# An expert layer whose second product moves 384 tokens past stationary weights, in place of 256 weight columns past stationary tokens

## The chip, the cores and the metric

The kernel runs on one core of a Trainium2 chip. The metric is the time of one execution on the device, in microseconds (us). TensorE is written PE in the profile (its weight loads PEld), VectorE DVE, ScalarE ACT, GpSimd POOL, SyncE SP.

## The reference, cut to what matters

Attention with keys and values pooled by 8 gives 2304 tokens of 512 channels, a dense layer pair (512 to 2048 to 512) follows, and then eight experts whose outputs are added under gates. The last part is the one that is changed:

```python
def _moe2_ref(x, w_gate, w1, w2):
    logits = x @ w_gate                       # 2304 x 8
    P = np.exp(logits - logits.max())
    for _ in range(8):
        P /= P.sum(1, keepdims=True) + 1e-09
        P /= P.sum(0, keepdims=True) + 1e-09
        P *= N / E
    out = np.zeros((N, D), dtype=np.float32)
    for e in range(E):                        # 8 experts
        h = np.maximum(x @ w1[e], 0.0)        # 512 -> 1024
        ye = h @ w2[e]                        # 1024 -> 512
        out += P[:, e:e + 1] * ye
    return out
```

## The kernel before

A float32 product is made on PE as three products of halves: each operand is split into a rounded high half and the low rest, and high by high, high by low and low by high are added in PSUM. The high half is a copy to the rounded type, mostly on ACT; the low half is a subtraction (operand less its high half) on DVE or POOL. The expert products moreover use a Strassen-Winograd scheme: seven block products with sums of blocks in place of eight.

The program has four stages: attention; the dense layers, item by item in a list `steps` of first-layer and second-layer pieces (matmuls in L663 and L698); the first pass over the experts; the second pass. Small jobs (the router, the Sinkhorn rounds, the splitting of weights) are generators in a list `side`, from which `advance()` takes one step at a time between products.

**First pass** (class `Unit`, matmul in L878). The tokens are 3 units `u` of 2 times 384. For each pair of 128-channel rows of an expert's hidden layer and each unit there are seven products of six matmuls, with 384 tokens moving. DVE and ACT combine them into seven forms of the hidden layer (B-side and A-side sums of the scheme), which SP writes to `hidden` in DRAM (`hid` in the trace).

**Second pass** (class `Pair`, matmul in L1092). It runs over 8 experts times 9 blocks `s` of 128 tokens, 72 pairs. A pair's forms come back from DRAM (`load_hidden`, tile `hl`), and `prepare` splits each form of 128 x 512: ACT writes the high half `g0` (L1057), and the low half `g1` (L1065) comes from POOL for two of the seven forms, from DVE through a copy in PSUM for three (ACT writes the copy `pg`, L1061), and from DVE straight for two. A product is 12 matmuls: 128 tokens of the form are stationary, 256 columns of `w2` move, and the result is token-major. `read` adds the products' banks (`poa` to `pod`) and `gated` multiplies by the gate, a scalar per partition, and adds to the accumulators `acc` in one instruction (L1109). After the last expert an accumulator is stored as it is (L1156). The seven products run in the order m1, m6, m3 of the pair before, m2, m7, m5, m4. Forms are split `AHEAD = 4` products ahead of their use; at the seam of the passes the first four are prepared by `first_weights` while the last units of the first pass run. The next expert's `w2` is loaded and split by `weights_ahead` (highs on ACT L994, lows on POOL L996, sums on POOL L987) one step for each product.

The very last product of the first pass, `last.product(3)`, follows the first product of the second pass.

Of the kernel before, what the change touches and what calls it, by code (L numbers as in the profile page):

```python
# [17 lines left out]
def tile_attention_mlp_moe(  # L18
# [539 lines left out]
    def gate_tile(t):  # L558
# [17 lines left out]
        yield  # L576
        ps = bank(f"pgt{t}")
# [16 lines left out]
    def sinkhorn():  # L594
# [17 lines left out]
        for it in range(8):  # L612
# [24 lines left out]
            yield  # L637


    side = []  # L640
# [215 lines left out]
    class Unit:  # L856
# [35 lines left out]
        def read(self, m):  # L892
# [7 lines left out]
            elif m == 2:  # L900
                self.r11 = self.temp("r11")
                nc.scalar.activation(self.r11, p["a"], AF.Relu)
                self.keep(H11, self.r11)
            elif m == 7:
                self.u3 = self.temp("u3")
                nc.vector.tensor_add(self.u3, p["b"], self.m1)
# [5 lines left out]
            elif m == 4:  # L912
                self.r12 = self.temp("r12")
                nc.vector.tensor_add(self.r12, p["d"], self.u3)
                nc.scalar.activation(self.r12, self.r12, AF.Relu)
                self.keep(H12, self.r12)
            else:

                c, s2 = p["c"], bank(f"ps_{self.i}_{self.u}")[:, 0:UW]
# [22 lines left out]
    w2s, loaded, prepared, acc = {}, {}, {}, {}  # L942
# [3 lines left out]
    pairs2 = [(e, u, s) for e in range(E) for u in range(NUNIT) for s in range(UB)]  # L946

# [4 lines left out]
    LOADS2 = (range(0, 4), range(4, 7))  # L952


    ON_POOL = (HS2, HS1)
    THROUGH_PSUM = (H11, H12, H22)

    POOLED = (H12, H22, 7 + H11, 7 + H12)
# [16 lines left out]
    def sum_w2(e, j, half):  # L975

        a, b = {T3: (T1, B22), T1: (T1, B11), T2: (B22, T1), T4: (B21, T2)}[j]
        if j == T3:
            if e == 0:
                out = piece([P, 2, HF], F32, f"t3_{half}")  # L980
            else:
                out = half_of(spare[0], half)
# [18 lines left out]
    def weights_ahead(e):  # L1001

        load_w2(e)
        for _ in range(8 if e > 1 else 12):
            yield
        for half in range(2):
            for j in (B11, B22, T3, B21, T1, T2, T4):
                if j in SUMS:
                    sum_w2(e, j, half)
                    yield  # L1010
                    yield
                yield from split_w2(e, j, half, nc.gpsimd)
                yield
                if j not in SUMS:
                    yield

    spare = []

    def last_acc():

        both = slot([P, SLOT], F32, "acc_t3")
        half = SLOT // 2
        acc[NTILE - 1] = both[:, 0:half].rearrange("p (s d) -> p s d", d=DM)
        spare.append(both[:, half:SLOT].rearrange("p (f d) -> p f d", f=NPAIR))

    next_load = [0]

    def load_hidden(forms):

        for _ in range(forms):  # L1030
            n, j = divmod(next_load[0], 7)
            next_load[0] += 1
            if n >= len(pairs2):
                return
            e, u, s = pairs2[n]
# [8 lines left out]
    def prepare(i):  # L1044
        run(prepare_steps(i))
# [465 lines left out]
```

## Time and profile before

| what | value |
|---|---|
| median of 3 runs | 1933.96 us (1933.7 to 1940.49) |
| the profiled execution: its own time | 1934.86 us |
| the profiled execution: span from first to last instruction | 1933.1 us |
| granted TensorE clock | 1.000 of full speed in all 40 slices |
| PE busy | 1906.9 us, 99% of the span |
| DVE, ACT, POOL busy | 70%, 56%, 38% |
| first matmul of the second pass starts | 1195.48 us |
| last group of 12 matmuls starts | 1926.52 us |

The span is the same execution's own time less 1.8 us that lie outside the first and last instruction. Durations below come from this execution. The trace pipelines matmuls: the time that a group of matmuls costs is read from the distance of the starts of two neighbouring groups, not from the printed length.

### The profile page before, as it was taken

The numbers are of one execution on the slowest core, as the hardware profiler recorded it, in microseconds if no ns is written. First come the engines' busy times: TensorE is split into PE (matmuls) and PEld (weight loads), VectorE is DVE, ScalarE is ACT, GpSimd is POOL, SyncE is SP. The second block draws the span as 40 slices with busy tenths as digits, with TensorE's granted clock in tenths as the row PEclk, the third lists the DMA queues.
The fourth block names the chain that finished last, engine by engine and source line by source line (L and its number), as shares of the span: only waits on it lengthen the run. The fifth ranks groups of instructions, "written<-read, shape, count | busy, mean of one in ns | idle before, by whom it ended". The sixth has DMA issues, their size and how long they took to land.

```text
span 1933.1 us, 35728 instructions
## 1 busy us (share of the span) xinstructions
PE 1906.9 (99%) x12635; PEld 1812.7 (94%) x12635; DVE 1356.4 (70%) x2557; ACT 1088.2 (56%) x2241; POOL 741.2 (38%) x658
## 2 busy tenths in 40 slices
PE   6999999999999999999999999999999999999998
PEld 4778888888999999999999999999999999999998
DVE  7778878456787666666666667557777777777766
ACT  7764545344544444444444446776666666666654
POOL 5700000010443333333333327566565656464621
PEclk9999999999999999999999999999999999999999
DMA  9421111000465556665566658876959495958675
GB/s 265 117 98 34 66 44 33 2 10 1 154 221 209 210 199 225 223 218 202 206 225 218 218 197 286 224 210 178 268 154 266 138 265 153 266 157 232 191 202 164
DMA packets 440163, 335.83 MB, mean 174 GB/s; under 512 B 25520, under 2 KB 431024, under 8 KB 439984
## 3 DMA queue, kind: packets, MB, share of 16 engines
q1 hardware_dynamic: 439984, 333.56, 55.8%
q8 instruction: 99, 1.62, 0.3%
q14 instruction: 80, 0.66, 0.1%
HBM read 196.62 MB, written 136.84 MB: 173 GB/s over the span
## 4 chain that ended last, share of the span: by engine, by line
PE 93%; DMA 2%; ACT 1%; POOL 1%; DVE 1%; issue 0%; SPq 0%; DVEq 0%; ACTq 0%; POOLq 0%
PE pb L878 10%; PE pa L878 10%; PE pc L878 10%; PE p L698 10%; PE poa L1092 10%; PE pob L1092 10%; PE poc L1092 10%; PE p L663 10%; PE pd L878 5%; PE pod L1092 5%; DMA hl<-hid 1%; POOL vraw L279 1%; DMA vraw<-in_v_dram 1%; PE px L425 1%; ACT g L1057 0%; PE pt L391 0%
## 5 line engine op out<-in xcount | busy, mean ns | idle before, releaser
L1057 ACT CAST g<-hl 128x512 fp32r<-128x512 f32 x504 | 304.6, 620 | 74.3 <-PE pob L1092 37.3
L1065 POOL TENSOR_TENSOR g<-hl,g 128x512 fp32r<-128x512 f32 x148 | 192.6, 1302 | 303.1 <-ACT g L1057 291.0
L849 POOL TENSOR_TENSOR w<-rw,w 128x512 fp32r<-128x512 f32 (+1 forms) x96 | 139.9, 1489 | 306.5 <-ACT w L847 211.9
L1092 PE MATMUL poa<-w,g 128*128 128x256 f32 x1728 | 232.3, 284 | 2.6 <-ACT n L1119 1.8
L1092 PE MATMUL pob<-w,g 128*128 128x256 f32 x1728 | 231.0, 283 | 0.0
L878 PE MATMUL pa<-xs,w 128*128 128x384 f32 x1152 | 230.9, 334 | 0.0
L1092 PE MATMUL poc<-w,g 128*128 128x256 f32 x1728 | 230.8, 283 | 0.0
L878 PE MATMUL pb<-xs,w 128*128 128x384 f32 x1152 | 230.8, 334 | 0.0
L878 PE MATMUL pc<-xs,w 128*128 128x384 f32 x1152 | 230.6, 334 | 0.0
L1092 PEld LDWEIGHTS poa<-w,g 128*128 128x128 f32 x1728 | 217.7, 192 | 4.9 <-ACT n L1119 3.5
L698 PE MATMUL p<-h,w 128*128 128x512 f32 (+1 forms) x960 | 215.8, 371 | 2.3 <-ACT h L686 1.9
L1092 PEld LDWEIGHTS pob<-w,g 128*128 128x128 f32 x1728 | 217.9, 192 | 0.1
L1092 PEld LDWEIGHTS poc<-w,g 128*128 128x128 f32 x1728 | 217.7, 192 | 0.0
L878 PEld LDWEIGHTS pb<-xs,w 128*128 128x128 f32 x1152 | 202.3, 188 | 0.3 <-DVE u L899 0.3
L878 PEld LDWEIGHTS pa<-xs,w 128*128 128x128 f32 x1152 | 202.2, 188 | 0.2
L878 PEld LDWEIGHTS pc<-xs,w 128*128 128x128 f32 x1152 | 202.4, 188 | 0.0
L698 PEld LDWEIGHTS p<-h,w 128*128 128x128 f32 x960 | 166.7, 189 | 36.8 <-ACT h L686 2.5
L841 POOL TENSOR_TENSOR rw<-rw 128x256 f32<-128x256 f32 x32 | 24.4, 762 | 419.1 <-DMA rw<-in_moe_w_dram 411.2
L1065 DVE TENSOR_TENSOR g<-pg,g 128x512 fp32r<-128x512 f32 x212 | 144.9, 684 | 49.2 <-ACT pg L1061 45.4
L938 ACT COPY s<-pc 128x384 f32<-128x384 f32 x96 | 46.2, 481 | 232.7 <-DVE ps L929 230.8
L663 PE MATMUL p<-xh,w 128*128 128x512 f32 x512 | 170.6, 393 | 0.0
L1065 DVE TENSOR_TENSOR g<-hl,g 128x512 fp32r<-128x512 f32 x144 | 132.7, 922 | 19.1 <-ACT g L1057 13.9
(186 smaller groups left out, 3292.2 us busy)
## 6 DMA issues: line engine op xcount, KB each, us to landing
hl<-hid SPq DMA_DIRECT2D x504, 256.0 KB, 5.2
hid<-s SPq DMA_DIRECT2D x384, 192.0 KB, 2.4
hid<-r SPq DMA_DIRECT2D x288, 192.0 KB, 2.6
rw<-in_moe_w_dram SPq DMA_DIRECT2D x128, 128.0 KB, 2.5
rv<-in_moe_w_dram SPq DMA_DIRECT2D x32, 512.0 KB, 7.1
raw<-in_moe_w_in_dram SPq DMA_DIRECT2D x16, 512.0 KB, 4.3
raw<-in_moe_w_out_dram SPq DMA_DIRECT2D x16, 512.0 KB
vraw<-in_v_dram SPq DMA_DIRECT2D x16, 288.0 KB
```

Source lines behind the costliest of these rows:

```text
L279: ins = nc.gpsimd.tensor_add(x[:, :, 0:n], x[:, :, 0:n], x[:, :, n : 2 * n])
L425: nc.tensor.matmul(ps[h * D : (h + 1) * D, :], vsum_of(u)[:, h * D : (h + 1) * D], turned_of(u, h), start=True, stop=True,)
L663: nc.tensor.matmul(ps[:, 0:n], wc[:, 0, a, c * P : (c + 1) * P], b[:, c, :], start=c == 0 and m == 0, stop=c == NC - 1 and m == 2,)
L698: nc.tensor.matmul(ps[j][:, 0 : WIDTH[t]], wc[:, 1, a, j * P : (j + 1) * P], h[b], start=f == 0 and m == 0, stop=f == SIZE[g] - 1 and m == 2,)
L841: g.tensor_sub(raw[:, S3], raw[:, A11], raw[:, A21])
L849: g.tensor_sub(w1s[i][1][:, js], raw[:, rs], f32(w1s[i][0][:, js]))
L878: nc.tensor.matmul(self.bank[b], a[:, c, :], x, start=first and c == 0 and n == 0, stop=c == 1 and n == 2, skip_group_check=not first,)
L938: nc.scalar.copy(v, x)
L1057: nc.scalar.copy(hi, x)
L1065: eng.tensor_sub(lo, x, f32(hi))
L1092: nc.tensor.matmul(self.bank[b], h[a][:, f, :], w2s[self.e, j][:, l, f, :], start=first and f == 0 and n == 0, stop=f == NPAIR - 1 and n == 2,
```

## The change

**Second pass** (class `Block` in place of `Pair`). It runs over 8 experts times 3 units, 24 blocks. A product's stationary operand is a chunk of 128 output channels of `w2`, and 384 tokens of the form move; the block of 256 channels is two chunks, each with a PSUM bank of its own, so a product is 2 x 12 matmuls and its result is channel-major. Forms are loaded and split in halves of 128 x 768 (two of the four 128-row pieces) in a ring: `load_half` fetches one, `high_half` is one ACT copy (L1088), and `low_half` is one subtraction in place (L1098): 9 of a block's 14 on DVE, 5 on POOL, none through PSUM.

**Gates.** The gate of a token now lies along the free axis. After Sinkhorn, two PE transposes, two ACT copies and 18 small DMAs write the gates as rows to `gate_rows` in DRAM; each block fetches two rows, spread over the 128 partitions (`gr`). `gated` is a multiplication and an addition on DVE (L1150, L1151); for the first expert it is one multiplication on DVE, where before it was an ACT instruction.

**Outputs.** The accumulators are channel-major (128 channels x 384 tokens). In the last expert `turn` transposes each unit's accumulators on PE (L1198), 72 transposes of 128 x 128, ACT copies the result to SBUF (L1204) and it is stored.

**Weights.** `weights_ahead` spreads the next expert's loads, sums and splits over about 42 calls of `advance`, and waits with the last three until the first product of the expert's last unit has been issued.

**Seam and dense layers.** At the seam nothing is split ahead any more; `first_weights` only loads. Two neighbouring entries of `steps` are exchanged, so that the first-layer piece of the last item of the dense layers runs one step earlier. Two more pauses stand in the router's generator, and the first pass releases its banks earlier.

```diff
+        yield from lull()
+        g = gates.rearrange("p s e -> p (s e)")
+        ps = bank("pgr")
+        nc.tensor.transpose(ps[:, 0:P], g[:, 0:P], ident)
+        nc.tensor.transpose(ps[0 : NS * E - P, P : 2 * P], g[:, P : NS * E], ident)
+        rows = piece([P, T], F32, "grows")
...
+                    nc.sync.dma_start(
+                        gate_rows[:, u, th, s * P : (s + 1) * P],
+                        rows[r : r + E, o * P : (o + 1) * P],
+                    )
...
-    ON_POOL = (HS2, HS1)
-    THROUGH_PSUM = (H11, H12, H22)
...
+    POOLED = {(6, 0), (2, 0), (3, 0), (4, 0), (5, 0)}
...
     def weights_ahead(e):
...
+        yield from load(B11, T1, 0)
+        yield from load(B22, B21, 0)
+        yield from load(B11, T1, 1)
+        yield from split(B11)
+        yield from load(B22, B21, 1)
+        yield from split(B22)
+        yield from sums(T3)
+        yield from split(T3)
+        yield from sums(T1, T2)
+        while last_of[0] < e:
+            yield
+        yield from split(T2, B21, T1)
+        yield from sums(T4)
+        yield from split(T4)
...
+    def load_half():
...
+            n, j, half = halves2[i]
+            ring[i] = slot([P, 2, 2, UW], F32R, f"hl{i}")
             nc.sync.dma_start(
...
+                f32(ring[i][:, 1]), hidden[blocks[n]][:, j, 2 * half : 2 * half + 2, :]
             )
...
+    def high_half():
...
+            nc.scalar.copy(ring[i][:, 0], f32(ring[i][:, 1]))
...
+    def low_half():
...
+            hi, lo = ring[i][:, 0], ring[i][:, 1]
+            eng = nc.gpsimd if (j, half) in POOLED else nc.vector
+            eng.tensor_sub(lo, f32(lo), f32(hi))
...
+    class Block:
...
+            for th in range(2):
+                g = piece([P, UW], F32, f"gr{n}_{th}")
+                one = gate_rows[self.e : self.e + 1, self.u, th, :]
+                nc.sync.dma_start(g, bass.AP(one.tensor, one.offset, [[0, P], [1, UW]]))
...
-        def product(self, j):
+        def product(self, j, halves=(0, 1), chunks=(0, 1)):
...
-                        h[a][:, f, :],
-                        w2s[self.e, j][:, l, f, :],
...
+            for half in halves:
+                h = ring[place2[self.n, j, half]]
+                for c in chunks:
+                    for f in range(2):
+                        for n, (l, x) in enumerate(((0, 0), (0, 1), (1, 0))):
+                            nc.tensor.matmul(
+                                self.bank[b][c],
+                                w2s[self.e, j][:, l, 2 * half + f, c * P : (c + 1) * P],
+                                h[:, x, f, :],
...
+        def gated(self, eng, th, dh, c, v):
+            y = self.y(th, dh, c)
             if self.e == 0:
-                nc.scalar.activation(y, v, AF.Copy, scale=gate)
+                eng.tensor_mul(y, v, self.gate[th])
             else:
-                nc.vector.scalar_tensor_tensor(y, v, gate, y, op0=ALU.mult, op1=ALU.add)
...
+                eng.tensor_mul(v, v, self.gate[th])
+                eng.tensor_add(y, v, y)
...
             elif m == 4:
...
+                for c in chunks:
+                    V.tensor_add(p["d"][c], p["d"][c], self.u3[c])
+                    self.gated(V, 1, 0, c, p["d"][c])
...
+        def turn(self, th, dhs=(0, 1), chunks=(0, 1), copy=None):
...
+                        nc.tensor.transpose(
+                            ps[s][:, cols[-1] : cols[-1] + P],
+                            self.y(th, dh, c)[:, s * P : (s + 1) * P],
+                            ident,
+                        )
...
+                (copy or nc.scalar.copy)(sb[:, s, ds], ps[s][:, ds])
...
+                    store(t, r, sb[:, s, :])
...
         steps += [(2, i - LAG)] if i - LAG >= N0 else []
+    ahead = steps.index((1, len(items) - 1))
+    steps[ahead - 1 : ahead + 1] = steps[ahead], steps[ahead - 1]
...
-        ahead = [prepare_steps(next(coming)) for _ in range(AHEAD)]
-        next(ahead[0])
...
     AHEAD = 4
...
+    def multiply(block, j):
...
+        for half in range(2):
+            i = place2[block.n, j, half]
+            last_one = min(i + AHEAD, len(halves2) - 1)
+            while next_low[0] <= last_one:
+                if next_high[0] <= next_low[0]:
+                    high_half()
+                low_half()
+            while next_high[0] <= min(i + AHEAD + 0, len(halves2) - 1):
+                high_half()
+            block.product(j, (half,))
+            load_half()
+            advance()
+        block.read(j)
...
+            for j in (0, 1, 6, 2, 3, 4, 5):
+                if j < 6:
+                    multiply(block, j)
...
+                if n == 0 and j == 0:
+                    last.product(3)
+                    w1s.clear()
...
+                if final and j == 0:
+                    before.turn(1)
+                if final and j == 3:
+                    before.turn(0)
...
+        block.product(6, chunks=(0,))
+        block.turn(1)
+        block.turn(0, dhs=(0,))
+        block.read(6, chunks=(0,))
+        block.product(6, chunks=(1,))
+        block.turn(0, dhs=(1,), chunks=(0,))
+        block.read(6, chunks=(1,))
+        block.turn(0, dhs=(1,), chunks=(1,))
```

ACT at the seam, before: `r22` and `r12` are the last ReLUs of the first pass, `g0` the high halves (number 4 is the fifth form), `n1` the read of the first product.

```order
L910 ACTIVATE r22_31_2_12976<-r22_31_2_12976 128x384
L915 ACTIVATE r12_31_2_12987<-r12_31_2_12987 128x384
L1057 CAST g0_4_12993<-hl0_1_12788 128x512
L1119 COPY n1_0_13010<-poa_0_12997 128x256
L1057 CAST g0_5_13018<-hl0_1_12788 128x512
L938 COPY s1_31_2_13047<-pc_31_2_12969 128x384
```

The same place in the changed kernel, where `hl0`, `hl1` and so on are the half forms and `u20`, `u21` the read of the first product.

```order
L931 ACTIVATE r22_31_2_12983<-r22_31_2_12983 128x384
L936 ACTIVATE r12_31_2_12994<-r12_31_2_12994 128x384
L1088 CAST hl0_12786<-hl0_12786 128x768
L1088 CAST hl1_12798<-hl1_12798 128x768
L1088 CAST hl2_12812<-hl2_12812 128x768
L1088 CAST hl3_12825<-hl3_12825 128x768
L1088 CAST hl4_12874<-hl4_12874 128x768
L1088 CAST hl5_12885<-hl5_12885 128x768
L1159 COPY u20_0_13044<-poa_0_0_13012 128x384
```

The high half that the first product needs stood further up among the first pass's copies; it now stands behind the last ReLU, and six casts stand ahead of the read of the first product.

DVE in the second pass, before: a pair's middle, with the lows `g1` between the reads of the banks.

```order
L1127 TENSOR_TENSOR v3_39_18919<-pob_39_18848,n1_39_18841 128x256
L1065 TENSOR_TENSOR g1_279_18924<-hl39_1_18673,g0_279_18923 128x512
L1130 TENSOR_TENSOR pc_39_18945<-poc_39_18932,v3_39_18919 128x256
L1065 TENSOR_TENSOR g1_282_18949<-pg282_18951,g0_282_18948 128x512
L1132 TENSOR_TENSOR pc_39_18945<-pod_39_18954,v3_39_18919 128x256
L1109 SCALAR_TENSOR_TENSOR acc1_13281<-pc_39_18945,gates_80,acc1_13281 128x512
```

The same products (m5 and m4) of a block in the changed kernel.

```order
L1175 TENSOR_TENSOR pt13_0_16932<-poc_13_0_16898,u30_13_16892 128x384
L1150 TENSOR_TENSOR pt13_0_16932<-pt13_0_16932,gr13_1_16696 128x384
L1151 TENSOR_TENSOR acc2_13501<-pt13_0_16932,acc2_13501 128x384
L1175 TENSOR_TENSOR pt13_1_16936<-poc_13_1_16899,u31_13_16893 128x384
L1150 TENSOR_TENSOR pt13_1_16936<-pt13_1_16936,gr13_1_16696 128x384
L1151 TENSOR_TENSOR acc3_13505<-pt13_1_16936,acc3_13505 128x384
L1098 TENSOR_TENSOR hl196_16889<-hl196_16889 128x768
L1098 TENSOR_TENSOR hl197_16912<-hl197_16912 128x768
L1179 TENSOR_TENSOR pod_13_0_16942<-pod_13_0_16942,u30_13_16892 128x384
L1150 TENSOR_TENSOR pod_13_0_16942<-pod_13_0_16942,gr13_1_16696 128x384
L1151 TENSOR_TENSOR acc2_13501<-pod_13_0_16942,acc2_13501 128x384
```

Each read is now two groups of an addition, a multiplication and an addition of 384 columns, and the two lows between them stand one behind the other.

PE at the end of the program, before: the last product's matmuls.

```order
L1092 MATMUL pod_71_23672<-w2_7_5_21787,g1_502_23606 128x256
L1092 MATMUL poc_71_23657<-w2_7_6_21357,g0_503_23626 128x256 x2
L1092 MATMUL poc_71_23657<-w2_7_6_21357,g1_503_23627 128x256
L1092 MATMUL poc_71_23657<-w2_7_6_21357,g0_503_23626 128x256 x2
L1092 MATMUL poc_71_23657<-w2_7_6_21357,g1_503_23627 128x256
```

The same end in the changed kernel, from the first chunk of the last product; `pt1` and `pt0` are the banks that receive transposes.

```order
L1124 MATMUL poc_23_0_19814<-hl334_19750,w2_7_6_18478 128x384 x6
L1124 MATMUL poc_23_0_19814<-hl335_19770,w2_7_6_18478 128x384 x6
L1198 MATMUL pt1_0_23_19894<-ident_72,acc4_13782 128x128 x4
L1198 MATMUL pt1_1_23_19895<-ident_72,acc4_13782 128x128 x4
L1198 MATMUL pt1_2_23_19896<-ident_72,acc4_13782 128x128 x4
L1198 MATMUL pt0_0_23_19917<-ident_72,acc3_13505 128x128 x2
L1198 MATMUL pt0_1_23_19918<-ident_72,acc3_13505 128x128 x2
L1198 MATMUL pt0_2_23_19919<-ident_72,acc3_13505 128x128 x2
L1124 MATMUL poc_23_1_19815<-hl334_19750,w2_7_6_18478 128x384 x6
L1124 MATMUL poc_23_1_19815<-hl335_19770,w2_7_6_18478 128x384 x6
L1198 MATMUL pt0_0_23_19917<-ident_72,acc3_13505 128x128
L1198 MATMUL pt0_1_23_19918<-ident_72,acc3_13505 128x128
```

18 transposes have come between the two chunks of the last product, and 6 behind it (two of them shown).

## Rows read from the trace of the kernel before

**Rows 1.** The page: busy time, granted clock, DMA share, and the critical chain.
```profile
PE 1906.9 (99%) x12635; PEld 1812.7 (94%) x12635; DVE 1356.4 (70%) x2557; ACT 1088.2 (56%) x2241; POOL 741.2 (38%) x658
...
PEclk9999999999999999999999999999999999999999
...
PE 93%; DMA 2%; ACT 1%; POOL 1%; DVE 1%; issue 0%; SPq 0%; DVEq 0%; ACTq 0%; POOLq 0%
```
**Rows 2.** Stretches of the second pass: PE busy (matmuls), clock, DMA share, GB/s.
```profile
1195.48:1220.00 24.52, 23.72 (x187) 1.00 1.06 328
1220.00:1240.00 20.00, 19.15 (x157) 1.00 1.16 289
...
1300.00:1600.00 300.00, 300.00 (x2502) 1.00 0.77 214
```
**Rows 3.** Timeline of PE, second pass: start, length, instructions.
```profile
1195.48 1.59 PE L1092 MATMUL poa<-w,g 128*128 128x256 f32 x12
...
1500.29 1.60 PE L1092 MATMUL poc<-w,g 128*128 128x256 f32 x12
1501.72 1.60 PE L1092 MATMUL pod<-w,g 128*128 128x256 f32 x12
...
1926.52 1.60 PE L1092 MATMUL poc<-w,g 128*128 128x256 f32 x12
```
**Rows 4.** Timeline of PE, first pass.
```profile
800.95 1.20 PE L878 MATMUL pd<-xs,w 128*128 128x384 f32 x6
801.99 1.20 PE L878 MATMUL pa<-xs,w 128*128 128x384 f32 x6
```
**Rows 5.** A later stretch, busy time and instructions: PE, PEld, DVE, ACT, POOL.
```profile
1500.00:1700.00 200.00, 200.00 (x1669) 200.00 (x1668) 143.44 (x258) 131.74 (x250) 116.17 (x90) 1.00 0.72 200
```
**Rows 6.** Timeline near the seam: ACT's last ReLU of the first pass.
```profile
1196.60 0.53 ACT L915 ACTIVATE r<-r 128x384 f32<-128x384 f32 x1
```
**Rows 7.** Casts on ACT, 560 to 1100 us, by shape: busy, mean ns.
```profile
L847 ACT CAST w<-rw 128x768 fp32r<-128x768 f32 x25 | 21.0, 839 | 26.6 <-PE pc L878 25.5 <-issue 1.0
```
**Rows 8.** DMA issues: KB each, median us from issue to landing.
```profile
hl<-hid SPq DMA_DIRECT2D x504, 256.0 KB, 5.2
```
**Rows 9.** Timeline of PE in the dense layers, the wait in brackets.
```profile
489.74 1.40 PE L698 MATMUL p<-h,w 128*128 128x256 f32 x7 [1.58 <-ACT h L686]
```
**Rows 10.** Timeline of PE in attention: four transposes and what follows.
```profile
64.67 0.60 PE L391 MATMUL pt<-ident,u 128*72 128x128 f32 x4
65.02 1.17 PE L698 MATMUL p<-h,w 128*128 128x512 f32 x4
```
**Rows 11.** Timeline of DVE at the end of the program.
```profile
1928.63 0.48 DVE L1109 SCALAR_TENSOR_TENSOR acc_t<-poc,gates,acc_t 128x256 f32<-128x256 f32 x1
```
**Rows 12.** DVE by shape: the first pass (560 to 1100), the second (1300 to 1900).
```profile
L921 DVE TENSOR_TENSOR pc<-pc,u 128x384 f32<-128x384 f32 x74 | 41.9, 566 | 30.5 <-PE pc L878 30.5
...
L1065 DVE TENSOR_TENSOR g<-pg,g 128x512 fp32r<-128x512 f32 x180 | 123.0, 683 | 23.9 <-ACT pg L1061 21.1 <-POOL g L1065 0.4
L1065 DVE TENSOR_TENSOR g<-hl,g 128x512 fp32r<-128x512 f32 x120 | 110.3, 919 | 0.0
```
**Rows 13.** POOL by shape, 560 to 1100 us, then 1300 to 1900 us.
```profile
L849 POOL TENSOR_TENSOR w<-rw,w 128x768 fp32r<-128x768 f32 x25 | 46.3, 1851 | 171.4 <-ACT w L847 163.4 <-PE pa L878 7.9
...
L1065 POOL TENSOR_TENSOR g<-hl,g 128x512 fp32r<-128x512 f32 x120 | 155.7, 1297 | 248.7 <-ACT g L1057 236.9 <-DMA hl<-hid 11.0
L996 POOL TENSOR_TENSOR w<-rv,w 128x512 fp32r<-128x512 f32 x72 | 93.5, 1299 | 23.7 <-ACT w L994 21.2 <-DMA hl<-hid 1.7 <-DVE g L1065 0.7
```
**Rows 14.** DVE's subtractions that read `hl`: minimum, median, maximum ns.
```profile
L1065 DVE TENSOR_TENSOR g<-hl,g x144: 679/683/1830, 1194.3 to 1921.8; 128x512 fp32r<-128x512 f32 x144
```
**Rows 15.** Timelines of DVE and POOL around 1622 us.
```profile
1621.79 1.61 DVE L1065 TENSOR_TENSOR g<-hl,g 128x512 fp32r<-128x512 f32 x1
...
1621.54 1.30 POOL L996 TENSOR_TENSOR w<-rv,w 128x512 fp32r<-128x512 f32 x1
1622.80 1.75 POOL L987 TENSOR_TENSOR acc_t<-rv,rv 128x512 f32<-128x512 f32 x1
```

More of the change, by code (lines that the diff above doesn't have):

```diff
@@ L1001, in weights_ahead, with rest_for, load @@
     def weights_ahead(e):
[L1003 to L1008 removed]
+        def rest_for(n):
+            for _ in range(n):
+                yield
+        def load(j0, j1, i):
+            if i == 0:
+                both[j0] = slot([P, 2, NPAIR, HF], F32, f"rv{e}_{j0}")
+            j = (j0, j1)[i]
+            hh, dh = {B11: (0, 0), T1: (0, 1), B21: (1, 0), B22: (1, 1)}[j]
+            rows = w2[e][hh * HALF : (hh + 1) * HALF, dh * HF : (dh + 1) * HF]
+            raw2[e, j] = both[j0][:, i]
+            nc.sync.dma_start(both[j0][:, i], rows.rearrange("(f p) d -> p f d", p=P))
+            yield
+            if not i:
+                yield
@@ L1009, in weights_ahead, with split, sums @@
+        def split(*js):
+            for j in js:
+                for half in range(2):
+                    more = split_w2(e, j, half, nc.gpsimd)
+                    next(more)
+                    yield
+                    run(more)
+                    yield
+        def sums(*js):
+            for j in js:
+                for half in range(2):
                     sum_w2(e, j, half)
                     yield
-                    yield
-                yield from split_w2(e, j, half, nc.gpsimd)
@@ L1013, in weights_ahead @@
[L1013 to L1031, printed above, removed]
-            next_load[0] += 1
-            if n >= len(pairs2):
-                return
-            e, u, s = pairs2[n]
-            part = int(j >= LOADS2[1].start)
-            js = LOADS2[part]
-            if j == js.start:
-                loaded[n, part] = slot([P, len(js), NPAIR, P], F32, f"hl{n}_{part}")
+        both = {}
@@ new lines, in product @@
+        def product(self, j, halves=(0, 1), chunks=(0, 1)):
+            m = ORDER2[j]
+            b = PRODUCTS[m][2]
+            first = PRODUCTS[m][3] or m == 7
+            if b not in self.bank:
+                self.bank[b] = [bank(f"po{b}_{self.n}_{c}")[:, 0:UW] for c in range(2)]
+            for half in halves:
[7 more added lines that the diff above has]
+                                h[:, x, f, :],
+                                start=first and half == 0 and f == 0 and n == 0,
+                                stop=half == 1 and f == 1 and n == 2,
+                                skip_group_check=m in (2, 3),
+                            )
+                if chunks[-1] == 1:
+                    del ring[place2[self.n, j, half]]
```

265 lines of the change are left out of this document (119 added, 146 removed).

## The prediction

> **What bounds the kernel now.** I read the busy shares and the clock of the page first: PE is busy 99% of the span at the full granted clock, 2.4 GHz, and holds 93% of the critical chain [rows 1]. So the time is a count of matmuls times what one costs, and the next view is the second pass by stretches. From 1300 to 1600 us PE runs 2502 matmuls in 300.0 us without a gap [rows 2]: 119.9 ns for a matmul with 256 moving columns. Two neighbouring groups of 12 start 1.43 us apart, which is the same [rows 3]. In the first pass, where 384 columns move past the same 128 x 128 weights, groups of six start 1.04 us apart [rows 4]: 173.3 ns. The reader should see that 1.5 times the columns cost 1.445 times the time. The slope is 53.4 ns for 128 columns, 0.417 ns each, which is one column per cycle at 2.4 GHz; what is left, 119.9 - 106.7 = 13.2 ns, is paid once per matmul whatever moves.
>
> The second pass runs from 1195.48 to 1926.52 + 1.44 = 1927.96 us [rows 3]: 732.5 us. Its 72 x 7 x 12 = 6048 matmuls take 725.1 of these, the six of the first pass's last product 1.0, and about 6.3 us are waits. Those lie at the start: the first 44.5 us hold 187 + 157 matmuls, some 41.2 us of work, while the DMA share stands at 1.06 and 1.16 [rows 2].
>
> The other engines have room: between 1500 and 1700 us DVE is busy 72%, ACT 66%, POOL 58% [rows 5].
>
> **The change, part by part.**
>
> *Matmuls.* 24 blocks x 7 products x 24 = 4032 matmuls with 384 columns, in place of 6048 with 256. The columns streamed are the same, 1,548,288; what goes is 2016 times the fixed part. 4032 x 0.1733 = 698.9 against 725.1: **-26.2 us**. The weights' width is 128 columns in both, so the shape is exactly that of the first pass, and the bounds are narrow (13 ns times 2016 is 26.6).
>
> [...]
>
> *Seam.* Before, the first product's operand was split early and PE went on at 1195.48. Now ACT's first cast stands behind the last ReLU, which ends at 1196.60 + 0.53 = 1197.13 [rows 6]. A cast of 768 takes 0.84 [rows 7], the low half behind it 0.92 (below), with hand-overs 1199.1: 3.6 us of wait where there was none. About 1 us more I allow for the following halves, whose casts run at 0.84 us against 2.08 us of PE work each. So about 4.5 us of waits take the place of 6.3: **-1.8 us**. Nothing in the trace shows the ring starting; the bounds are no wait at all (-6.3) and 10 us of it (+3.7), if the loads behind a DMA share over 1 come late (a load takes 5.2 us to land [rows 8], and the ring reads the same bytes).
>
> *Steps of the dense layers.* The exchange removes the one wait of 1.58 us before the second-layer matmuls at 489.74 [rows 9]: **-1.6 us**, or 0 if what ACT has queued there only moves the wait.
>
> *Gate rows.* Four transposes of 128 x 128 advance PE by 0.35 us (64.67 to 65.02) [rows 10], 87.5 ns each; two of them are **+0.2 us**. Their two copies and 18 DMAs, and the 48 loads of 192 KB, lie on ACT and SP some 600 us ahead of the pass, or beside 29 us of PE work; uncovered, one row load would cost as much as a form's load, 5.2 us, once.
>
> *Transposes of the outputs.* 66 stand ahead of the last product's end: 66 x 0.0875 = **+5.8 us**. Twice, in the last two blocks, `turn(1)` follows the next block's first product and needs the accumulations of m4, six DVE operations that are queued behind lows; I take a wait of 1.0 us each, **+2.0 us** (bounds 0.4 and 2.5 each).
>
> *Tail.* Before, from the last matmul's end (1927.96) to the end of the span (1933.1) it is 5.1 us: an addition and a gate on DVE until 1929.11 [rows 11], then 4.0 for the store. Now let T be the end of product m4 of the last block. DVE then has six operations, 3.5 us; 12 transposes 1.1 (T + 4.6), six more 0.5, the second chunk of the last product 2.1 (T + 7.2), its three DVE operations 1.7 (T + 8.9), three transposes and three short ACT copies 0.9 (T + 9.8), and the store 4.0: T + 13.8. With the last product's 4.16 and 1.6 of transposes already counted, 8.0 us are left after them: **+2.9 us** (bounds +1 and +6).
>
> Sum: -26.2 - 1.8 - 1.6 + 0.2 + 5.8 + 2.0 + 2.9 = -18.7. Against the profiled execution, 1934.86 us, that is 1916.2; that execution lies 0.9 above the median of the runs, so 1915.3 on their scale. I predict 1916.
>
> *What must stay hidden.* A block is 168 x 0.1733 = 29.1 us of PE. **DVE** has 26 reads of 384 columns in a block (from the second expert on), 0.566 each by the nearest row [rows 12]: 14.7 us. The scalar gate of one instruction has become a multiplication and an addition, and the copies in PSUM are gone. Its nine lows of 768: 512 columns take 0.683, 384 columns 0.566 [rows 12], so 768 take about 0.92: 8.3 us. That is 23.0 of 29.1, if nothing slows the lows. **POOL** has five lows of 1.85 and a third of the weights' work (14 splits of 1.30 and 8 sums, taken at the same) [rows 13]: 9.3 + 9.5 = 18.8 us, 65%. **ACT** has 14 casts of 0.84 [rows 7], a third of the weights' 14 at no more than that, and two reads of about 0.53 [rows 6]: 11.8 + 3.9 + 1.1 = 16.8. In order, each product needs its halves four halves ahead; the tightest are those issued between the reads of m5 and m4, which are ready about 2 us after product m1 of the following block starts and are needed after 4.2 or later. So none of the three should hold PE, but DVE is the one near it.
>
> *What slows the lows.* A subtraction that reads two SBUF operands has a median of 0.683 and a maximum of 1.83 us [rows 14], a mean of 0.919 where those that read PSUM keep 0.683 [rows 12]. At 1621.79 one took 1.61 us: POOL's split ran to 1622.84, the subtraction ended 0.6 behind it, and POOL's next operation took 1.75 [rows 15], against 1.30 of its neighbours. They exclude one another. The change turns the lows that read PSUM into lows that read SBUF. The mean wait is 0.919 - 0.683 = 0.24 at a POOL share of 58% and operations of 1.30; with 65% and 1.85 it becomes 0.24 x 1.12 x 1.42 = 0.38: 3.4 us a block, DVE at 26.4 of 29.1 us, 91%. It decides at (29.1 - 23.0) / 9 = 0.68 us of wait for each low.
>
> [...]
>
> **The rivals.**
>
> *Small waits in each block* (chance 0.15). Reads now stand in pairs of three operations, so a bank comes free some 1.7 us later than one read of before; with the two lows behind, PE could wait half a microsecond per block. Against it: eight banks and the slack above. 24 x 0.5 = 12 us more: 1928.
>
> *DVE becomes the bound through POOL* (0.08), the case on the other side. If every low meets half a POOL operation, 0.93, DVE needs 14.7 + 9 x 1.85 = 31.4 us a block, 2.3 more than PE; over the 21 blocks that have a gated addition 48 us: 1964. From a wait of 0.68 it binds, and from 0.83 (1.35 us a block, 28.4 in all) the kernel is more than 0.5% slower. For it: the maximum of 1.83 in rows 14. Against: the measured mean.
>
> *The fixed part is not saved* (0.03): 384 columns past `w2` cost 106.7 x 1.5 plus as much as three halves of the fixed part, and only about 5 us come off: 1937. Against it stands the first pass with the same shape.
>
> *Seam or tail are 10 us longer* (0.08), by late loads: 1926.
>
> *Better than forecast* (0.08): no waits at the seam and before the transposes, and a tail as before: 1916.2 - 4.5 - 2.0 - 2.9 = about 1907.
>
> **How the numbers follow.** The forecast, 1908 to 1924 around 1916, has the rest, 0.58. I take 0.5% (9.7 us) as what this kernel's measurement can tell from no change: faster is below 1924.3, slower above 1943.6. Faster gets the forecast, the better case, and the lighter thirds of the small waits and of the seam: 0.70. Slower is the DVE case and a little of the others: 0.10; the rest, 0.20, is the same. The range takes in the forecast, the small waits, the longer seam and the lower end of the bounds: 1908 to 1935, and leaves out half of the better case, the DVE case and part of the fixed-part case.
>
> **What would show it.** Right: groups of six L1124 matmuls 1.04 us apart in the steady part, PE without gaps from about 1205 us on, about 709 us from the first L1124 matmul to the last, no bracketed wait near 490 us, DVE's lows of 768 at 0.92 in the median and below 1.6 in the mean, DVE busy near 90%. Wrong: idle before L1124 released by DVE's L1098 or by its reads (small waits or the DVE bound), by the load of `hl` (seam), or a spacing of six above 1.1 us.

## The result and the profile after

The changed kernel takes 1917.08 us (median of 4 runs, 1914.32 to 1918.23); before, beside it, 1935.65. The ratio is 0.990, 95% interval 0.9888 to 0.9912: faster by 1.0%, clear of the 0.5% that the prediction took as the least that can be told. The prediction was 1916, range 1908 to 1935. The profiled execution has a time of 1917.55 and a span of 1915.8 us, 17.3 shorter than before's.

On the page, PE is busy 1890.2 us (99% of the span), DVE 1499.2, ACT 964.2 and POOL 854.0 us. The page's clock row still reads full, as in [rows 1], though the mean granted clock of the execution is 0.997.

The timeline of PE in the steady part of the second pass, which answers to [rows 3]:

```profile
1500.12 4.32 PE L1124 MATMUL poa<-hl,w 128*128 128x384 f32 x24
1504.28 4.32 PE L1124 MATMUL pob<-hl,w 128*128 128x384 f32 x24
```

24 matmuls in 4.16 us are 173.3 ns each, without a gap, which is the spacing behind the main term, -26.2 us.

PE's timeline at the seam:

```profile
1192.78 1.21 PE L899 MATMUL pd<-xs,w 128*128 128x384 f32 x6
1195.96 0.69 PE L1124 MATMUL poa<-hl,w 128*128 128x384 f32 x1 [1.97 <-ACT hl L1088]
1196.95 6.93 PE L1124 MATMUL poa<-hl,w 128*128 128x384 f32 x23 [0.30 <-DVE hl L1098]
1203.72 1.20 PE L899 MATMUL pc<-xs,w 128*128 128x384 f32 x6
1204.76 4.32 PE L1124 MATMUL pob<-hl,w 128*128 128x384 f32 x24
```

A stretch there (us, PE busy with the matmuls in it, granted clock, DMA share, GB/s):

```profile
1198.00:1202.00 4.00, 4.00 (x14) 0.50 0.90 224
```

From 1192.78 to 1204.76, 11.98 us, stand 36 matmuls, 6.24 us of work at 173.3 ns. So 5.7 us are lost here: 2.3 in the two waits in brackets, 2.8 because the 23 matmuls behind them run for the most part at a granted clock of 0.50 (14 in 4 us) and take 6.77 us for 3.99, and the remaining 0.7 in the ends of the matmuls before each wait, which nothing overlaps (0.17 and 0.52 by the lengths above, less 1.04 and 0.17).

How long the clock stays low differs from execution to execution. Seven profiled kernels have this seam unchanged: from `pd` to `pob` three of them take 12.0 to 12.1 us (the changed kernel, e4_pool8, e10_pool0) and four 10.8 to 10.9. e5_pool3 is one of these four, with a granted clock of 1.00 from 1202 to 1206 us, where the changed kernel has 0.90; in the same stretch as above:

```profile
1198.00:1202.00 4.00, 4.00 (x16) 0.57 0.95 226
```

Nothing like it stands in before, where PE never waited so long in the pass (0.7 us at the longest). The waits of PE there, and one of them with what ACT did ahead of it:

```profile
PE poa L1092 <- ACT n L1119: 1.8, 4, 0.5
PE poa L1092 <- DVE g L1065: 0.7, 1, 0.7
...
1242.16 0.69 ACT L1107 ACTIVATE acc<-pc,gates 128x512 f32<-128x512 f32 x1 [1.70 <-DVE pc L1132]
...
1243.25 0.38 ACT L1119 COPY n<-poa 128x256 f32<-128x256 f32 x1
...
1243.68 1.69 PE L1092 MATMUL poa<-w,g 128*128 128x256 f32 x12 [0.43 <-ACT n L1119]
```

Added up from start to start of its matmuls, the second pass of before has lost nothing by 1205 us, 3.4 us by 1240 and 5.8 of its 6.3 by 1300. So most of the 6.3 us is not the start of the second pass but is spread over the nine pairs of the first expert: there ACT makes the gate's multiplication (L1107), waits for DVE with it, and the read `n` that PE needs is queued behind. One wait, the 0.7 for DVE, comes from a load: ACT had waited 2.29 us for `hl`, up to 1215.29. The change took the gate's multiplication off ACT.

Then the end of the pass and the tail, on PE:

```profile
1841.24 0.27 PE L1198 MATMUL pt<-ident,acc 128*128 128x128 f32 x1
1842.14 1.42 PE L1198 MATMUL pt<-ident,acc 128*128 128x128 f32 x11 [0.63 <-DVE acc L1151]
1843.32 4.41 PE L1124 MATMUL pob<-hl,w 128*128 128x384 f32 x24
...
1860.05 1.47 PE L1198 MATMUL pt<-ident,acc 128*128 128x128 f32 x12
1861.28 4.42 PE L1124 MATMUL poc<-hl,w 128*128 128x384 f32 x24
1865.54 4.32 PE L1124 MATMUL pod<-hl,w 128*128 128x384 f32 x24
...
1901.48 2.24 PE L1124 MATMUL poc<-hl,w 128*128 128x384 f32 x12
1903.57 0.27 PE L1198 MATMUL pt<-ident,acc 128*128 128x128 f32 x1
1904.28 2.07 PE L1198 MATMUL pt<-ident,acc 128*128 128x128 f32 x17 [0.44 <-DVE acc L1151]
1906.11 2.35 PE L1124 MATMUL poc<-hl,w 128*128 128x384 f32 x12
```

The first group of transposes costs 2.08 us, three further groups 1.23 each (one shown), the 18 inside the last product 2.54: 8.3 us, 0.4 less than what the pass is longer than its matmuls from 1204.76 on (1906.11 - 1204.76 = 701.35, less 3996 x 0.1733 = 692.6). These 0.4 stand in the product behind each group, which takes about 4.26 us for 4.16 (1861.28 to 1865.54). The last product ends at 1908.19, the span 7.6 later.

DVE's and POOL's lows between 1300 and 1850 us by shape, the answer to [rows 12, 13], and POOL's splits of the weights:

```profile
L1098 DVE TENSOR_TENSOR hl<-hl 128x768 fp32r<-128x768 f32 x169 | 277.5, 1667 | 13.1 <-ACT hl L1088 12.9
...
L1098 POOL TENSOR_TENSOR hl<-hl 128x768 fp32r<-128x768 f32 x94 | 193.5, 2062 | 94.8 <-ACT hl L1088 88.8 <-PE poc L1124 5.5
L1007 POOL TENSOR_TENSOR w<-rv,w 128x512 fp32r<-128x512 f32 x72 | 125.5, 1743 | 36.3 <-ACT w L1005 36.3
```

A low on DVE takes 1.67 us in the mean where the shortest take 0.94; it was forecast at 1.30. POOL's own operations are longer too: the splits take 1.74 us where before's took 1.30, the lows 2.06 for the forecast 1.85. Between 1300 and 1850 us, 138 of DVE's 169 lows start within a POOL operation, and they end 0.81 to 0.85 us behind that operation's end; in before 38 of 110 subtractions that read `hl` start so and end 0.54 to 0.65 behind it, and the other 72 take 0.68. POOL's splits that start within a low of DVE take 2.01 us in the median, the others 1.29. Yet PE waits for none of them in the steady part.

### The profile page after: what moved, and what is told of

It reads as the page before. It is cut to its first block, busy times and chain, and to the rows that moved or that the text cites. A ratio compares the mean times of both kernels' runs of the same rounds, so it can differ in the third digit from the quotient of the medians.

```text
span 1915.8 us, 30959 instructions
## 1 busy us (share of the span) xinstructions
PE 1890.2 (99%) x10693; PEld 1796.2 (94%) x10693; DVE 1499.2 (78%) x2468; ACT 964.2 (50%) x1836; POOL 854.0 (45%) x630
## 4 chain that ended last, share of the span: by engine, by line
PE 93%; DVE 3%; POOL 1%; DMA 1%; ACT 1%; issue 0%; SPq 0%; ACTq 0%; DVEq 0%
PE pb L899 10%; PE pa L899 10%; PE pc L899 10%; PE p L719 10%; PE p L684 10%; PE poa L1124 10%; PE pob L1124 10%; PE poc L1124 10%; PE pd L899 5%; PE pod L1124 5%; DVE hl L1098 1%; PE px L425 1%; POOL vraw L279 1%; PE pt L391 0%; DMA vraw<-in_v_dram 0%
## 5 line engine op out<-in xcount | busy, mean ns | idle before, releaser
L1098 DVE TENSOR_TENSOR hl<-hl 128x768 fp32r<-128x768 f32 x216 | 343.6, 1614 | 44.0 <-ACT hl L1088 43.5
L1088 ACT CAST hl<-hl 128x768 fp32r<-128x768 f32 x336 | 276.1, 837 | 201.2 <-DMA hl<-hid 189.4
L1098 POOL TENSOR_TENSOR hl<-hl 128x768 fp32r<-128x768 f32 x120 | 249.7, 2084 | 155.0 <-ACT hl L1088 138.7
L1124 PE MATMUL poa<-hl,w 128*128 128x384 f32 x1152 | 210.7, 337 | 2.3 <-ACT hl L1088 2.0
L1124 PE MATMUL poc<-hl,w 128*128 128x384 f32 x1152 | 207.9, 334 | 0.0
L1124 PE MATMUL pob<-hl,w 128*128 128x384 f32 x1152 | 207.6, 334 | 0.0
L1124 PEld LDWEIGHTS poa<-hl,w 128*128 128x128 f32 x1152 | 203.1, 190 | 3.0 <-ACT hl L1088 2.3
L1124 PEld LDWEIGHTS pob<-hl,w 128*128 128x128 f32 x1152 | 200.3, 188 | 0.0
L1124 PEld LDWEIGHTS poc<-hl,w 128*128 128x128 f32 x1152 | 200.3, 188 | 0.0
L1007 POOL TENSOR_TENSOR w<-rv,w 128x512 fp32r<-128x512 f32 x92 | 156.1, 1700 | 41.7 <-ACT w L1005 41.7
```

What stands on the lines that cost most here:

```text
L1007: eng.tensor_sub(lo, x, f32(hi))
L1088: nc.scalar.copy(ring[i][:, 0], f32(ring[i][:, 1]))
L1098: eng.tensor_sub(lo, f32(lo), f32(hi))
L1124: nc.tensor.matmul(self.bank[b][c], w2s[self.e, j][:, l, 2 * half + f, c * P : (c + 1) * P], h[:, x, f, :], start=first and half == 0 and ...
```

## The experiments

Each time is a median, against 1917.08 of the changed kernel; every kernel is the changed one with one edit (e8_seam2 with two). The runs of one kernel differ by up to 5.5 us (those of before by up to 6.8), so a difference of 3 us or less is read from the traces.

**Narrower matmuls (e1_width192).**

```diff
-                                h[:, x, f, :],
...
+                            for q in range(0, UW, UW // 2):
...
+                                    h[:, x, f, q : q + UW // 2],
```

> Each matmul of the second pass that moves 384 tokens is split into two that move 192, with the same weights loaded for each: 8064 matmuls for 4032, the same columns. If every matmul has a fixed part of 13.2 ns, as the two widths of before showed, neighbours stand 80.0 + 13.2 = 93.2 ns apart, and the pass grows by 4032 x 13.2 = 53 us: 1970 us. [...] A third way: the weight load of 128 columns sets a floor, as the 12 transposes of the changed kernel suggest (1.23 us, 102 ns each): then 8064 x 0.1025 = 827 us for 699, 2045 us.

Measured: 2116.49 us. 48 matmuls stand in 5.35 us, 111.5 ns each:

```profile
1500.59 5.52 PE L1125 MATMUL pob<-hl,w 128*128 128x192 f32 x48
1505.94 1.28 PE L1125 MATMUL poc<-hl,w 128*128 128x192 f32 x10
```

That is the way with a floor, of 111 ns in place of 102. So this run doesn't measure the fixed part at all.

**The widths by themselves (e9_widths).**

```diff
+        for n in (512, 384, 512, 448, 384, 320, 256, 192, 128):
+            ps = bank("width")
+            for k in range(24):
...
+                    xs[:, 0:n],
```

> Behind the last transposes PE runs nine more groups of 24 matmuls on operands that lie in SBUF, nothing of which is used: 512 and 384 columns first, then 512, 448, 384, 320, 256, 192 and 128, each matmul with a weight load of 128 columns of its own. Theory: from 256 columns up two starts stand N / 2.4 + 13.2 ns apart (119.9, 146.5, 173.3, 199.9, 226.5), which is the line through before's two widths, so the saving of the change is a fixed part times the matmuls that went; below 256 the weight load sets a floor near 111 ns, the spacing that the run with 192 columns showed, so that 192 and 128 take the same. [...]

Measured in one execution (1947.43 us with the added matmuls) from start to start, with the other engines idle: 226.6 ns for 512 columns (the settled part of the group), 202.7 for 448, 173.4 for 384 (settled part), 146.3 for 320, 119.8 for 256, 110.9 for 192, 110.3 for 128. The view of these matmuls by shape (mean ns of one record) has the same steps, some 27 ns for 64 columns from 512 down to 256, then 10, then none:

```profile
...
L1552 PE MATMUL width<-w,w 128*128 128x512 f32 x24 | 5.6, 391 | 0.0
L1552 PE MATMUL width<-w,w 128*128 128x448 f32 x24 | 5.0, 365 | 0.0
L1552 PE MATMUL width<-w,w 128*128 128x320 f32 x24 | 3.7, 309 | 0.0
L1552 PE MATMUL width<-w,w 128*128 128x256 f32 x24 | 3.0, 283 | 0.0
L1552 PE MATMUL width<-w,w 128*128 128x192 f32 x24 | 2.8, 273 | 0.0
L1552 PE MATMUL width<-w,w 128*128 128x128 f32 x24 | 2.8, 273 | 0.0
```

The theory holds on both counts: N / 2.4 + 13.2 ns from 256 up (448 lies 2.8 above that line, the others within 0.2), and 110 to 111 ns at 192 and 128. With the other engines idle 256 and 384 columns take 119.8 and 173.4 ns, in the passes 119.9 and 173.3, so the 13.2 ns are not the work of what runs beside them. Every matmul here has a weight load of its own, so how much of the 13.2 ns is the load's is not shown; that the load makes the floor at 192 and 128 is the author's estimate.

**The transposes left out (e3_no_turn).**

```diff
-                        nc.tensor.transpose(
...
-                (copy or nc.scalar.copy)(sb[:, s, ds], ps[s][:, ds])
+                    nc.sync.dma_start(slab(r), self.y(th, dh, c))
```

> The 72 transposes and their copies are left out; the channel-major accumulators are stored as they are, so the output's rows are not in the reference's order. Theory: four groups of 12 transposes at 1.23 us, the 2.5 us of 18 before the last chunk, and some 1.5 us of the tail go: 9.0 us, 1908. By the terms of the prediction (5.8 + 2.0 + 2.9) it would be 10.7 us, 1906. Rival: the transposes stood where PE would have waited for DVE anyway, and under 4 us go: above 1913.

Measured: 1906.99 us, 10.1 less. In the trace, `pob` starts at 1205.38 us and the pass's last matmul 694.55 us later, which is 4007 spacings of 173.3 ns with nothing lost; the changed kernel takes 703.36 for the same matmuls. Behind the start of the last matmul stand 5.03 us for 7.65. That makes 8.8 and 2.6, 11.4 together, against the prediction's 7.8 (5.8 and 2.0) and 2.9: its terms are confirmed, the rival is out.

**The seam (e2_seam_ahead, e6_fill, e7_last_first, e8_seam2).** First the four halves split ahead (the pair of calls stands three times, and one more `low_half()` ends them):

```diff
+        high_half()
         yield
         load_half()
+        low_half(), high_half()
```

> The first four half forms are split before the seam again (ACT and DVE or POOL work is issued among the last steps of the first pass). Theory: the changed kernel lost 5.7 us at the seam, 2.3 of them waiting for the first cast and the first low half, the rest because TensorE's granted clock stood at half after that wait, so both go: first matmul of the second pass at about 1193.9 in place of 1195.96, no stretch at half clock, 1911.4 us. Rival: the splitting takes the place of the first pass's own reads on ACT and DVE, and PE waits there instead: 1915 to 1917.

Measured: 1917.89 us: the rival. DVE's and POOL's timelines, then PE's:

```profile
1186.29 3.33 DVE L1098 TENSOR_TENSOR hl<-hl 128x768 fp32r<-128x768 f32 x2
...
1190.01 1.55 DVE L1098 TENSOR_TENSOR hl<-hl 128x768 fp32r<-128x768 f32 x1
1191.48 0.54 DVE L930 TENSOR_TENSOR r<-pc,u 128x384 f32<-128x384 f32 x1
...
1184.29 6.45 POOL L1007 TENSOR_TENSOR w<-rv,w 128x512 fp32r<-128x512 f32 x4
...
1192.08 1.32 PE L899 MATMUL pc<-xs,w 128*128 128x384 f32 x6 [2.79 <-DVE r L930]
1194.39 2.29 PE L899 MATMUL pa<-xs,w 128*128 128x384 f32 x6 [0.98 <-ACT m L917]
1196.47 2.12 PE L899 MATMUL pb<-xs,w 128*128 128x384 f32 x6
...
1194.00:1198.00 4.00, 3.61 (x11) 0.50 0.52 192
```

Two lows of 0.94 take 3.33 us against POOL's splits and a third 1.55, the first pass's read L930 comes late, and PE waits 2.79 us there; behind it six matmuls advance PE by 2.08 us, twice their 1.04, at a granted clock of 0.50. The wait had only moved, and the clock fell with it.

Next, PE is kept busy in the wait: `bank` issues the number of matmuls that stands in `busy` ahead of a bank's first use.

```diff
             block = Block(n)
+            busy[0] = 20 if n == 0 else 0
```

> 20 matmuls of the identity, 128 columns each (about 2 us by the 0.1 us that such matmuls stand apart), are issued on PE ahead of the second pass's first product, in the time in which it waits for the first cast. They compute nothing that is used. Theory: the granted clock halved because PE stood idle there; kept busy it stays at full, and of the 5.7 us lost at the seam the 3.4 that 24 matmuls at half clock cost are saved: 1913.7 us. Rival: the clock falls by itself or by a load that comes from elsewhere: a stretch at half clock remains and the time is 1917.

Measured: 1916.08 us. PE's timeline:

```profile
1194.74 4.63 PE L103 MATMUL poa<-ident 128*128 128x128 f32 x40
1199.12 4.41 PE L1124 MATMUL poa<-hl,w 128*128 128x384 f32 x24
1203.37 1.20 PE L899 MATMUL pc<-xs,w 128*128 128x384 f32 x6
...
1198.00:1202.00 4.00, 4.00 (x30) 1.00 0.83 240
```

No stretch at half clock: the 24 matmuls take 4.25 us, where they took 7.76 from 1195.96 (0.30 of it a wait). I mis-sized the filling: 20 matmuls are 40 on PE and last 4.38 us, 2 more than the wait, so most of the gain went into them; the median is 1.0 less, which the runs can't tell from nothing. The theory on the clock holds.

Then the first pass's last product is moved ahead of the second pass's first:

```diff
+                if n == 0 and j == 0:
+                    last.product(3)
+                    w1s.clear()
                 if j < 6:
                     multiply(block, j)
```

> The first pass's last product (six matmuls, 1.04 us) is issued ahead of the second pass's first product in place of behind it. Theory: PE's wait at the seam shrinks from 2.3 to 1.2 us; if the granted clock then stays at full, 4.4 us are saved, 1912.7; if it halves still, 1.0: 1916. Rival: the product must wait itself, for the bank that DVE reads: nothing is saved.

e8_seam2 has this edit and two casts ahead in the last steps of the first pass:

```diff
         load_half()
+        high_half()
         yield
+        high_half()
         yield
```

> As the run with the last product first, and besides the casts of the first two half forms (ACT only, no subtraction) are issued among the first pass's last ReLUs. Theory: the first product then waits only for the first low half on DVE, ready about 1.7 us after the last unit's product m4; 1.04 are covered, about 0.7 us of wait is left and the clock does not halve: 5 us saved, 1912 us. Rival: the two casts delay the first pass's copies on ACT, as the splitting ahead did on DVE, and PE waits there: 1915 to 1918.

Measured: 1914.62 and 1915.24 us. PE's timelines at the seam, first of e7_last_first, then of e8_seam2:

```profile
1196.36 1.21 PE L899 MATMUL pd<-xs,w 128*128 128x384 f32 x6
1197.43 1.32 PE L899 MATMUL pc<-xs,w 128*128 128x384 f32 x6
1199.54 0.44 PE L1124 MATMUL poa<-hl,w 128*128 128x384 f32 x1 [0.79 <-ACT hl L1088]
1200.53 4.26 PE L1124 MATMUL poa<-hl,w 128*128 128x384 f32 x23 [0.56 <-DVE hl L1098]
1204.63 4.32 PE L1124 MATMUL pob<-hl,w 128*128 128x384 f32 x24
```

```profile
1193.40 1.21 PE L899 MATMUL pd<-xs,w 128*128 128x384 f32 x6
...
1195.67 4.72 PE L1124 MATMUL poa<-hl,w 128*128 128x384 f32 x24
1200.23 4.32 PE L1124 MATMUL pob<-hl,w 128*128 128x384 f32 x24
```

From the last unit's product to `pob` it is 8.27 and 6.83 us, where the changed kernel takes 11.98: 3.7 and 5.15 saved, near the theory's 4.4 and 5; the granted clock is 1.00 from 1194 to 1206 us in both. Against the four executions in which the unchanged seam takes 10.8 to 10.9, it is 2.6 and 4.0. The medians show 2.5 and 1.8 less, within the intervals (ratios to before 0.9885, 0.9868 to 0.9901, and 0.9889, 0.9874 to 0.9904). That these two beat the changed kernel is not settled; that they beat before is.

**Who makes the lows (e4_pool8, e5_pool3, e10_pool0).**

```diff
-    POOLED = {(6, 0), (2, 0), (3, 0), (4, 0), (5, 0)}
+    POOLED = {(6, 0), (2, 0), (3, 0), (4, 0), (5, 0), (1, 1), (3, 1), (5, 1)}
```

> POOL makes 8 of a block's 14 low halves in place of 5, DVE 6 in place of 9. Theory: what counts is the time in which DVE's lows and POOL's operations exclude one another. With 5 on POOL that is 9 x 0.94 + 5 x 1.84 + 9.5 = 27.2 of a block's 29.1 us; with 8 it is 6 x 0.94 + 8 x 1.84 + 9.5 = 29.9, 0.8 more than PE needs: some 17 us over 22 blocks, 1934, with PE waiting for lows on POOL. Rival: only DVE's own time counts (26 reads and the lows at the 1.63 us that they took); it falls from 29.2 to 24.3 us a block and POOL alone has room, so the time stays at 1917 and DVE's busy share falls to about 85%.

> POOL makes 3 of a block's 14 low halves in place of 5, DVE 11 in place of 9. With 8 on POOL (the run before) DVE's lows waited longer each (1.78 us for 1.67), but there were fewer, and PE hardly waited. Theory: DVE's own time is the near limit; 26 reads at 0.555 and 11 lows at 0.94 are 24.8 us of a block's 29.1, and a low that still waits as long as now, 0.7, makes it 32.5; with POOL at 15.0 us of work a block in place of 18.7 I expect a wait of 0.5 and 30.3 us: 1.2 over PE's time in some 22 blocks, 26 us, 1943, with PE waiting for lows on DVE. Rival: the waits are elastic, that is they fill what time DVE has left and give way when it has none; the work itself, 24.8 us, fits, so the time stays at 1917.

> All 14 low halves of a block are on DVE; POOL keeps only the weights' work, 9.5 us a block. With 3 lows on POOL the lows' mean fell from 1.67 to 1.46 us, DVE was busy 97.5%, and the pass grew by 3 us. Theory: waits give way as far as they can, but the work itself now nears PE's 29.1 us: 26 reads at some 0.5 (back to back they overlap) and 14 lows at 0.9 are 25.6, and of POOL's 9.5 us some part stands in the way of DVE; if a third to a half of it does, 29 to 30.5 us a block, so 0 to 1.4 us over PE's time in 22 blocks: 1920 to 1947 us, PE waiting for DVE's lows in most blocks. Rival: DVE's waits were never near PE's path, and the time stays within 2 us of 1917.

Measured in one execution each, busy shares and lows from 1300 to 1850 us; the pass is from the start of the first `pob` to that of the last L1124 matmul (702.5 to 703.4 in six other kernels with the split of 9 and 5):

| lows on DVE, POOL | median us | pass | DVE busy | POOL busy | mean low on DVE |
|---|---|---|---|---|---|
| 6, 8 | 1920.3 | 705.8 | 82% | 92% | 1.78 |
| 9, 5 (changed kernel) | 1917.08 | 703.4 | 95% | 76% | 1.67 |
| 11, 3 | 1918.79 | 706.3 | 98% | 60% | 1.46 |
| 14, 0 | 1939.84 | 726.0 | 98% | 38% | 1.26 |

With no low on POOL, the wait of PE that costs most (total us, times, longest):

```profile
PE poc L1124 <- DVE hl L1098: 7.8, 16, 0.7
...
```

And the stretch of that kernel (busy: PE, PEld, DVE, ACT, POOL):

```profile
1300.00:1850.00 550.00, 536.39 (x3046) 526.81 (x3046) 540.15 (x720) 266.91 (x377) 210.19 (x132) 1.00 0.73 219
```

The first theory (the sum of work that excludes each other) failed: with 8 on POOL it asked for 17 us, and the pass grew by 2.4. The second, DVE's own time, stands with a correction. The wait of a low, its mean less 0.94, is 0.84, 0.73, 0.52 and 0.32 us, so in these four executions it goes with POOL's busy share. That waits simply give way when DVE has no time left, the rival of e5_pool3, fits the run with 11 lows but not the one with 14: there the work alone, 25.6 us by its expectation, would fit into PE's 29.1, and yet a low waits 0.32 and PE loses a microsecond a block. And back to back DVE's records overlap (in the changed kernel three reads of 0.55 to 0.57 take 1.66 us from the first's start at 1500.37 to the next instruction's, and a low of 1.67 is followed after 1.59), so DVE had more room than the sum of durations says. At 8 lows on POOL PE begins to wait for POOL (0.5 us for one low), at 11 on DVE DVE is full and PE loses 3 us, at 14 DVE is the bound and the kernel is no faster than before (1.0016, 1.0006 to 1.0025). By the pass, the changed kernel's 9 stand at the best of the four; by the medians only the run with 14 is clearly slower.

**The exchange undone (e11_no_swap).**

```diff
-    ahead = steps.index((1, len(items) - 1))
-    steps[ahead - 1 : ahead + 1] = steps[ahead], steps[ahead - 1]
```

> The changed kernel without the exchange of the two steps of the dense layers. Theory: the wait of 1.58 us of PE for ACT before the second-layer matmuls, near 490 us, is there again and the exchange's wait of 0.25 is gone: the last dense matmul starts some 1.3 us later against the first unit's steps, 1918.4 us, too little for the medians to show, so the row of PE's timeline decides. Rival: with the router's added pauses the wait would not have come back, 1917.1, and no bracket of over 0.5 us stands there.

Measured: 1917.87 us. The rows of PE, first without the exchange, then the changed kernel's:

```profile
489.63 0.86 PE L719 MATMUL p<-h,w 128*128 128x256 f32 x5 [0.85 <-DVE h L708]
```

```profile
489.34 2.65 PE L719 MATMUL p<-h,w 128*128 128x256 f32 x20 [0.25 <-DVE h L708]
```

Neither: the wait comes back at 0.85, not at 1.58. From the start of the last 12 matmuls with 512 columns to that of the first pass's first `pd`, PE takes 20.20 us without the exchange (478.26 to 498.46), 19.42 with it (477.79 to 497.21) and 21.12 in before (478.32 to 499.44). So of the 1.7 us that went here, the exchange is worth 0.8. The other 0.9 is by other edits ahead, of which the router's pauses are one; they were not tried apart.

## Why the prediction was right, step by step

- **Matmuls, -26.2:** as forecast. The spacing was read from the first pass of before, and e9_widths shows that the fixed part belongs to the matmul with its weight load and not to its surroundings; e3_no_turn runs 4007 of these spacings in a row. The case in which it isn't saved is out; no run shows the 5 us that it takes off, and the runs show 13.2 ns for each of 2016 matmuls, 26.6 us. The traces give the clock only as a share of full speed; what the rows show of the prediction's 2.4 GHz is 2.4 columns a nanosecond, one over its slope of 0.417 ns a column, which e9_widths repeats (226.6 less 119.8 ns for 256 columns more).
- **Seam, -1.8:** the first matmul waits as the sum said, for the cast behind the last ReLU (ready 3.2 us after the last unit's product starts, 2.3 of waits). What the step left out is the clock: 2.8 us at half clock here, less in other executions, while the further microsecond for the following halves didn't come. 5.7 lost against 4.5 forecast, by partly wrong terms. The 6.3 of before that it was set against were misread: they do not lie at the start, and of the waits that are named there, 1.8 are for ACT's reads in the first expert and 0.7 comes from a load. So the -0.6 is 5.7 more at the seam and 6.3 less behind it, mostly in the first expert, whose gate moved from ACT to DVE; that the two nearly cancel, as forecast, is luck. That the gate's move is what took them away is argued from the rows, not tried apart.
- **Steps of the dense layers, -1.6:** the stretch there is 1.7 us shorter (21.12 and 19.42), but only 0.8 of it is the exchange. Up to the first pass's last product the kernel is 1.7 us ahead as well (1194.44 before, 1192.78 after); that number is of two executions, and kernels with the same code up to there reach this product between 1192.6 and 1196.4 us, so the 0.2 for the gate rows can't be read from it.
- **Transposes and waits, +5.8 and +2.0:** 8.7 measured with the products behind, against 7.8: a group of 12 takes 1.23 for the 1.05 of the sum and 1.33 with the 0.1 in the product behind it, 111 ns each, which is what e9_widths shows at 128 columns. The row that the price came from had four transposes between other work. One of the two waits came (0.63), the other not.
- **Tail, +2.9:** 7.6 for 5.1, +2.5. T was 1901.48, so the end was forecast at 1915.3 and came at 1915.8: the step's chain was right, and the 0.5 beyond it is near the 0.44 us wait inside the last group of transposes.
- Together: -1.7 - 26.2 - 0.6 + 8.7 + 2.5 = -17.3, the difference of the spans; forecast -18.7.
- **What must stay hidden:** this step was mis-sized, and that it did no harm is luck. The wait for a low was forecast at 0.38 us and came at 0.73; the sign named for it, lows of 0.92 in the median and below 1.6 in the mean, did not come (medians of 1.67, means of 1.61 in the whole pass and 1.67 between 1300 and 1850 us). Put into the sum's own formula, POOL's measured 76% and 1.85 us an operation give 0.45, so the formula itself falls short; why is open. 0.68 was named as the point where DVE binds. The wait passed that point without binding, since two errors cancel: the sum of durations counted the overlap of DVE's records twice. DVE was busy 98% between 1500 and 1700 us (195.2 of 200), not 91. So DVE as the bound was nearer than its 0.08 said: five lows more than the changed kernel's 9 make it so, and the gain is gone.
- **Small waits in each block:** none; PE runs 1300 to 1600 us with 300.0 busy.

## What to carry to other kernels

Count matmuls, not only columns: where every matmul loads 128 columns of weights, it cost about 13 ns beside its columns from 256 moving columns up, and 110 to 111 ns at 192 and at 128 alike, so the operand with the longer free axis should move. Look at what stands ahead of a read that PE waits for: in before it was ACT's gate multiplication, which itself waited 1.70 us for DVE. When the operands of DVE's subtractions move to SBUF, price them with the wait behind POOL's operations (0.73 us a low here, with POOL busy 76%) and find by a neighbouring split (a few more, a few fewer) where DVE binds. A wait of two microseconds on PE at a seam can cost more than itself, by the clock (here 2.3 us of waits, and 2.8 more at a granted clock of 0.50); move independent matmuls into it before splitting operands ahead, which may only move the wait (to 2.79 us in e2_seam_ahead).

## What the runs showed of the hardware that was not expected

With 2.3 us of idle PE and one matmul between, the granted clock fell to half (0.50 between 1198 and 1202 us in the changed kernel), and 23 matmuls took 2.8 us longer. In e5_pool3, behind waits of 1.98 and 0.55 us in the same place, it was back at full sooner (0.57 in the same stretch, 1.00 behind it), and the seam took 1.1 us less. With PE kept busy in the same place it stayed at full (1.00 in e6_fill), and with waits of 0.79 and 0.56 us too (1.00 in e7_last_first). A subtraction of 0.94 us on DVE took up to 2.61 us beside POOL.
